# P x V of two heads in one group, in 32-column slices, and its banks in one common ring

## The chip, the cores and the metric

The kernel runs on one core of a Trainium2 chip. The metric is device time in microseconds (us) of one execution; several executions of a kernel are taken and their median is compared. A core has five engines that run their own instruction queues in order and wait for each other through semaphores: TensorE (PE, matrix products; its weight loads are shown as PEld), VectorE (DVE), ScalarE (ACT), GpSimd (POOL) and SyncE (SP, which here issues the DMAs).

## The reference

Attention with a soft cap over 4 x 12 heads of 448 x 64, then two MLPs on 1792 tokens of width 768. The second MLP multiplies two branches, and its last two weights are applied one after the other.

```python
scores = scale * np.matmul(q, k.transpose(0, 1, 3, 2))
scores = cap * np.tanh(scores / cap)
attn = np.exp(scores - np.max(scores, axis=-1, keepdims=True))
attn = attn / (np.sum(attn, axis=-1, keepdims=True) + 1e-09)
x = np.matmul(attn, v)                    # per head; heads side by side: 1792 x 768
h = x @ w_in                              # first MLP, d_ff 2048
x = (h * np.cos(h)) @ w_out
h = (x @ w1) * (x @ w2) @ w3              # second MLP, d_ff 1024
out = h @ w_out2
```

## The kernel before

**Attention.** Heads are taken in 24 pairs. For each head the 448 keys are four chunks of 112, taken two at a time, so a pair has four score blocks. A score block (`c_S`, L615 and L616) is four matmuls into a double bank; ScalarE turns it into tanh and then exp (`c_exp`, L625), and the exponentials land in a tile p of 112 keys x 2 chunks x 448 queries. The ring of p has four tiles. P x V (`c_PV`, L627) is one planned operation for two chunks of both heads, twice per pair. It multiplies with V as the weight (64 columns for each head; the two heads fill the two halves of a bank, L639) and with 32 columns of ones, which gives the sums of the exponentials in a second bank, one strip of 32 partitions for each head and chunk (L643). These matmuls are in plain f32, and the profile shows each of them as two records. `c_move` copies both banks to SBUF (xs and zs), `c_sums` brings the sums together through small DMAs, inverts them (L665) and spreads them over the partitions by way of DRAM, `c_norm` multiplies (x, L369), and `a_out` splits x into a high and a low part for the products that follow, or sends both to DRAM for later.

**Beside it.** In the first part of the attention (until about 190 us) PE also forms the product of the two last weights (`make_w34`, tiles w2 and w3). Then the first MLP starts on the heads that are done (`moe1`): H blocks (xh, xl with wih, wil) give h, a chain on the other engines makes g out of it, and Y blocks (g with woh, wol) are added up in y by DVE, one bank after the other. Every product of this part is three matmuls of split operands (`mm3`, L383 to L385). The second MLP (`moe2`) follows.

**PSUM.** Eight banks: two doubles (four banks) for scores, bank 4 for P x V, bank 5 for the sums, banks 6 and 7 (`hy_r`) for all other products. When attention is over, its banks go to `hy_r`.

**What sets the order.** All operations are recorded in a plan with a due time and with the engines that may run them. `schedule` simulates the engines with fixed costs and picks, at each moment, the ready operation with the earliest due time; a tile of a ring is given out in the order of the ring's queue. The result is one fixed instruction order per engine. Due times of the attention come from `at(g)`, where g counts score blocks: 3.03 us apart for the first 48, then 5.82. P x V of two chunks is due with g at 3 and 5 after the first block of its pair, the copies at 6, `c_norm` at 10 and `a_out` at 11 (lag 9 of its second head, which starts two blocks later).

Of the kernel before, what the change touches and what calls it, by code (L numbers as in the profile page):

```python
# [19 lines left out]
P = 128  # L20
# [52 lines left out]

class Ring:
    def __init__(self, plan, pool, tag, shape, dtype, n, shift=0):
        self.pool, self.tag, self.shape, self.dtype, self.shift = pool, tag, list(shape), dtype, shift
        self.tiles, self.queue = {}, []
        self.free = [(0.0, k) for k in range(n)]
        plan.rings.append(self)
        pool.rings.append(self)  # L80
# [55 lines left out]
class Plan:  # L136
# [57 lines left out]
    def schedule(self):  # L194
# [23 lines left out]
        while done < len(self.ops):  # L218
# [4 lines left out]
            idle = {e for e in free if free[e] <= t + 1e-9}  # L223
            wait, rest, again = {}, [], False
            for c in cands:
# [6 lines left out]
                if pick[0] in idle and port(pick) and free["port"] > t + 1e-9:  # L232
                    pick = None
                elif pick[0] not in idle:
                    if len(o.opts) == 1:
                        wait[pick[0]] = wait.get(pick[0], 0.0) + pick[1] * PAR["back"]
                    pick = None
                if pick is None or any(it.slot is None and it.first is not o for it in o.uses if it.ring) or any(
                        it.ring.queue[0] is not it or not it.ring.free or it.ring.free[0][0] > t + 1e-9
                        for it in o.allocs):  # L240
                    rest.append(c)
                    continue
                for it in o.allocs:
                    it.ring.queue.pop(0)
                    it.slot = heapq.heappop(it.ring.free)[1]
# [88 lines left out]
def program(  # L334
# [70 lines left out]

    class Banks(Ring):
        def __init__(self, slots):
            Ring.__init__(self, plan, pools["psum"], "bank", [P, 512], F32, 0)
            self.free = [(0.0, k) for k in slots]
# [3 lines left out]

    class Doubles(Banks):
        def tile(self, k):
            return doubles[k]
# [42 lines left out]
    if general:  # L459
        s_r, pt_r, pv_r, hy_r = Banks((0, 1)), Banks((2, 3)), Banks((4, 5)), Banks((6, 7))  # L460
    else:
        s_r, pv_r, z_r, hy_r = Doubles((0, 1)), Banks((4,)), Banks((5,)), Banks((6, 7))

# [46 lines left out]
    else:  # L510
        tiles += [("v", [CP, 2, NC, D], F32, 2), ("ones", [CP, Q], F32, 1)]
        tiles += [("p", [CP, 2, S], F32, 4), ("xs", [P, S], F32, 2), ("zs", [P, S], F32, 2), ("rs", [P, 2, S // D], F32, 2), ("rb", [P, S], F32, 1)]
    for tag, shape, dtype, n in tiles:
# [38 lines left out]

    def a_out(i, g):

# [5 lines left out]
        if general:  # L560
            tt(at(g), x, Ref(rb.pop(i // 2)), x, S, ALU.mult, "PD")
        if b < BH:
# [3 lines left out]
        else:  # L566
            th, tl = A["xsh"].ref(), A["xsl"].ref()
        copy(at(g), th, x, S, "PAD")
        lo(at(g), tl, x, th, S)
        if b >= BH:  # L570
            for d, t in zip(xB_d, (th, tl)):
                z = d.at((b, kk), lambda d: d[b - BH, kk])
                dma(at(g + 1), z, t.view(lambda x: x.bitcast(F32)), r=[t], w=[z], kb=230, write=True)

# [52 lines left out]

    def c_PV(n, c, one, g):
        ps = [ph_t.pop((2 * n + j, c)) for j in range(2)]
        if c == 0:  # L630
            pv_t[n], zs_t[n] = pv_r.ref(), z_r.ref()
        pv, z, w = pv_t[n], zs_t[n], Ref(vt[n])
        flags = dict(start=c == 0, stop=c == NT - 1)

        def f():
            for k in range(2):
                first = dict(start=c == 0 and k == 0, stop=c == NT - 1 and k == 1)
                for j, p in enumerate(ps):
                    PE.matmul(pv()[j * D:(j + 1) * D, :S], w()[:, j, 2 * c + k], p()[:, k, :], **first)  # L639
            for j, p in enumerate(ps):  # L640
                for k in range(2):
                    q = Q * (2 * j + k)
                    PE.matmul(z()[q:q + Q, :S], one(), p()[:, k, :], **flags)  # L643

        plan.op(at(g), [("PE", 3 * 4 * MM, f)], r=[w, one, *ps], w=[pv, z])

# [26 lines left out]

    def c_norm(n, g):
        x32[n] = A["x32"].new()
        tt(at(g), Ref(x32[n]), pv_t.pop(n), Ref(rb[n]), S, ALU.mult, "DP")

# [5 lines left out]
    def columns():  # L683
# [3 lines left out]
        for g in range(-8, NT * NH + 16):  # L687
# [3 lines left out]
            if 0 <= g < NT * NH:  # L691
# [12 lines left out]
        plan.move(pv_r, hy_r, at(g))  # L704
        plan.move(z_r, hy_r, at(g))

# [113 lines left out]
    def queries():  # L820
        a_load(0, -2)
        a_split(0, -1)
        for g in range(-8, NC * NH + 24):
# [14 lines left out]
            of_head(a_R, 8, g, NC)  # L838
            of_head(a_out, 17, g, NC)
            if g == NC * G["hsw"] + 11:  # L840
# [513 lines left out]
```

## Time and profile before

| | us |
|---|---|
| median of 3 runs | 1092.33 (1091.08 to 1095.45) |
| the profiled execution | 1093.39 |
| its span in the trace | 1091.1 |
| PE busy | 1064.5 |
| DVE busy | 869.6 |
| ACT busy | 502.1 |
| POOL busy | 161.1 |

The span is the time from the first to the last instruction that was profiled; the execution's own time is 2.3 us more. The mean granted clock of TensorE is 0.997 of full speed. Line numbers are those of the kernel before. A matmul's record lasts longer than the time after which the next one may start, so the cost of a matmul in a row of them is the distance of two starts.

### The profile page before, as it was taken

The page shows a single profiled execution, that of the slowest core. Times are in us where ns is not written, and L with a number is a line of the kernel's source. Part 1 is how long each engine was busy: PE and PEld are TensorE (multiplying, and loading weights), DVE is VectorE, ACT ScalarE, POOL GpSimd, SP SyncE. Part 2 cuts the span into 40 slices and gives each one's busy share as a digit, 9 for nine tenths or more (in the row PEclk, how much of TensorE's full clock was granted, in tenths as well). Part 3 has the DMA queues.
Part 4 walks back from the last instruction along what each step waited for, and adds up shares of the span by engine and source line. Part 5 has one row for each costly group of instructions (what it writes and reads, how often), then busy time and mean ns, then how long its engine had stood idle before and what let it go on. Part 6 is the DMA issues. An engine that isn't in the chain of part 4 may idle for free.

```text
span 1091.1 us, 14889 instructions
## 1 busy us (share of the span) xinstructions
PE 1064.5 (98%) x5424; PEld 892.4 (82%) x5424; DVE 869.6 (80%) x1336; ACT 502.1 (46%) x661; POOL 161.1 (15%) x154
## 2 busy tenths in 40 slices
PE   5999999999999999999999999999999999999997
PEld 3666766677767777779999999998999999999996
DVE  6888767698978988969889977779799879667643
ACT  5788767787666656632244221112333236221121
POOL 2222111122312311111001110001223100000000
PEclk9999999999999999999999999999999999999999
DMA  8796876767756655425643422104655436321232
GB/s 244 200 221 181 231 209 174 219 208 223 219 161 197 188 171 166 153 84 193 223 141 119 147 58 59 58 15 136 223 188 203 141 104 226 119 87 59 59 96 95
DMA packets 83268, 169.17 MB, mean 155 GB/s; under 512 B 19698, under 2 KB 56562, under 8 KB 83186
## 3 DMA queue, kind: packets, MB, share of 16 engines
q1 hardware_dynamic: 83186, 168.14, 51.0%
q8 instruction: 44, 0.72, 0.3%
q14 instruction: 38, 0.31, 0.1%
HBM read 129.30 MB, written 38.62 MB: 154 GB/s over the span
## 4 chain that ended last, share of the span: by engine, by line
PE 90%; DVE 6%; ACT 2%; DMA 1%; issue 1%; SPq 0%; POOL 0%; DVEq 0%; POOLq 0%; ACTq 0%
PE bank L383 25%; PE bank L384 24%; PE bank L385 24%; PE bank L639 6%; PE double L615 3%; PE bank L643 3%; PE double L616 3%; DVE y L369 1%; DVE w L369 1%; DMA wi_d<-wx 1%; ACT double L625 1%; DVE kk L1008 0%; ACT p L625 0%; DMA kr<-in_k 0%; DVE g L369 0%
## 5 line engine op out<-in xcount | busy, mean ns | idle before, releaser
L383 PE MATMUL bank<-g,woh 128*128 128x448 f32 x384 | 140.8, 367 | 4.1 <-DVE y L369 3.5
L384 PE MATMUL bank<-g,woh 128*128 128x448 f32 x384 | 139.4, 363 | 0.9 <-DVE g L369 0.9
L383 PE MATMUL bank<-xh,wih 128*128 128x448 f32 x384 | 140.2, 365 | 0.0
L369 DVE TENSOR_TENSOR y<-bank,y 128x448 f32<-128x448 f32 x168 | 103.5, 618 | 45.7 <-PE bank L385 44.5
L385 PE MATMUL bank<-xh,wil 128*128 128x448 f32 x384 | 139.3, 363 | 0.0
L385 PE MATMUL bank<-g,wol 128*128 128x448 f32 x384 | 139.3, 363 | 0.0
L384 PE MATMUL bank<-xl,wih 128*128 128x448 f32 x384 | 139.2, 363 | 0.0
L359 ACT COPY hs<-bank 128x448 f32<-128x448 f32 x77 | 41.2, 535 | 200.9 <-PE bank L385 200.7
L625 ACT ACTIVATE double<-double,ts 112x896 f32<-112x896 f32 x96 | 94.0, 981 | 69.4 <-PE double L616 69.1
L625 ACT ACTIVATE p<-double,pac 112x896 f32<-112x896 f32 x96 | 96.6, 1012 | 1.8
L383 PEld LDWEIGHTS bank<-g,woh 128*128 128x128 f32 x384 | 71.9, 187 | 20.1 <-DVE y L369 6.2
L615 PE MATMUL double<-qh,ks 128*112 128x448 f32 x192 | 72.6, 378 | 13.9 <-DVE ks L369 9.6
L383 PEld LDWEIGHTS bank<-xh,wih 128*128 128x128 f32 x384 | 71.9, 187 | 16.0 <-issue 8.0
L639 PE MATMUL bank<-p,v 112*64 112x448 f32 x384 | 84.1, 558 | 0.0
L384 PEld LDWEIGHTS bank<-g,woh 128*128 128x128 f32 x384 | 72.1, 188 | 6.4 <-DVE g L369 1.3
L384 PEld LDWEIGHTS bank<-xl,wih 128*128 128x128 f32 x384 | 72.1, 188 | 5.2
L385 PEld LDWEIGHTS bank<-g,wol 128*128 128x128 f32 x384 | 72.1, 188 | 4.2
L385 PEld LDWEIGHTS bank<-xh,wil 128*128 128x128 f32 x384 | 72.1, 188 | 4.2
L616 PE MATMUL double<-ql,ks 128*112 128x448 f32 x192 | 72.3, 376 | 0.0
L384 PE MATMUL bank<-ab,w34h 128*128 128x448 f32 x192 | 69.7, 363 | 0.0
L383 PE MATMUL bank<-ab,w34h 128*128 128x448 f32 x192 | 69.7, 363 | 0.0
L385 PE MATMUL bank<-ab,w34l 128*128 128x448 f32 x192 | 69.3, 361 | 0.0
(224 smaller groups left out, 2304.4 us busy)
## 6 DMA issues: line engine op xcount, KB each, us to landing
rawc<-in_w_out SPq DMA_DIRECT2D x16, 768.0 KB, 5.1
stq<-w_d SPq DMA_DIRECT2D x32, 384.0 KB, 3.3
qr<-in_q SPq DMA_DIRECT2D x48, 224.0 KB, 4.2
kr<-in_k SPq DMA_DIRECT2D x48, 224.0 KB, 4.5
rawc<-in_w_in SPq DMA_DIRECT2D x13, 768.0 KB, 5.4
raw<-in_w3T SPq DMA_DIRECT2D x16, 512.0 KB, 5.9
rawl<-in_w SPq DMA_DIRECT2D x10, 768.0 KB, 4.7
raw<-in_w_out SPq DMA_DIRECT2D x8, 768.0 KB, 7.3
```

The source lines that it names most:

```text
L359: "A": ("ACT", (0.051 if psum else 0.094) + n / 1200, lambda: ACT.copy(dst(), src())),
L369: "D": ("DVE", 0.068 + n / 960, lambda: DVE.tensor_tensor(dst(), a(), b(), op=op))
L383: PE.matmul(out, wh, xh, start=first, stop=False, skip_group_check=on)
L384: PE.matmul(out, wh, xl, start=False, stop=False, skip_group_check=on)
L385: PE.matmul(out, wl, xh, start=False, stop=last, skip_group_check=on)
L615: PE.matmul(o, w, qh(), start=True, stop=False)
L616: PE.matmul(o, w, ql(), start=False, stop=True)
L625: lambda f=f, x=x, o=o: ACT.activation(o(), s(), f, scale=x[:CP]))],
L639: PE.matmul(pv()[j * D:(j + 1) * D, :S], w()[:, j, 2 * c + k], p()[:, k, :], **first)
L643: PE.matmul(z()[q:q + Q, :S], one(), p()[:, k, :], **flags)
```

## The change

Three things change together.

1. P x V of a pair is one operation for all four chunks (`cs` is `[0, 1]`), except for the first two pairs, which keep one operation for every two chunks. V goes in by 32 columns: for each chunk four matmuls (two heads, two halves of V) fill the four strips of a bank, so a pair has 16 V matmuls of 32 columns in place of 8 of 64. The matmuls with ones are the same as before and follow those with V. The planned cost on PE goes from 2.4 to 5.1 us for a whole pair's operation (12 x 2 x 0.2 + 0.3). The p ring has six tiles.
2. Banks 4 to 7 form one ring `hy_r` for P x V, the sums and all other products. In this ring (`loose`) a bank is given to whichever operation is ready, not in the order of the queue; an operation that needs two takes both or waits, and others behind it don't take one from under it (`short`).
3. `c_norm` is due 11 us and `a_out` 14 us after the copies, in place of some steps of g; the DMA of x to DRAM is due 3 us after `a_out`.

```diff
 class Ring:
+    loose = False
...
+                need = {}
+                for it in o.allocs:
+                    need[it.ring] = need.get(it.ring, 0) + 1
+                lack = {r for r, n in need.items() if sum(x[0] <= t + 1e-9 for x in r.free) < n}
                 if pick is None or any(it.slot is None and it.first is not o for it in o.uses if it.ring) or any(
-                        it.ring.queue[0] is not it or not it.ring.free or it.ring.free[0][0] > t + 1e-9
-                        for it in o.allocs):
+                        not r.loose and r.queue[0].first is not o for r in need) or lack or short & need.keys():
+                    short |= {r for r in lack if r.loose}
                     rest.append(c)
                     continue
                 for it in o.allocs:
-                    it.ring.queue.pop(0)
+                    it.ring.queue.remove(it)
...
     class Banks(Ring):
+        loose = not general
...
-        s_r, pv_r, z_r, hy_r = Doubles((0, 1)), Banks((4,)), Banks((5,)), Banks((6, 7))
+        s_r, hy_r = Doubles((0, 1)), Banks((4, 5, 6, 7))
...
-        tiles += [("p", [CP, 2, S], F32, 4), ...
+        tiles += [("p", [CP, 2, S], F32, 6), ...
...
-                dma(at(g + 1), z, t.view(lambda x: x.bitcast(F32)), r=[t], w=[z], kb=230, write=True)
+                dma(due + 3, z, t.view(lambda x: x.bitcast(F32)), r=[t], w=[z], kb=230, write=True)
...
-    def c_PV(n, c, one, g):
-        ps = [ph_t.pop((2 * n + j, c)) for j in range(2)]
-        if c == 0:
-            pv_t[n], zs_t[n] = pv_r.ref(), z_r.ref()
+    def c_PV(n, cs, one, g):
+        ps = {(j, c): ph_t.pop((2 * n + j, c)) for j in range(2) for c in cs}
+        if 0 in cs:
+            pv_t[n], zs_t[n] = hy_r.ref(), hy_r.ref()
         pv, z, w = pv_t[n], zs_t[n], Ref(vt[n])
-        flags = dict(start=c == 0, stop=c == NT - 1)
 
         def f():
-            for k in range(2):
-                first = dict(start=c == 0 and k == 0, stop=c == NT - 1 and k == 1)
-                for j, p in enumerate(ps):
-                    PE.matmul(pv()[j * D:(j + 1) * D, :S], w()[:, j, 2 * c + k], p()[:, k, :], **first)
-            for j, p in enumerate(ps):
-                for k in range(2):
-                    q = Q * (2 * j + k)
-                    PE.matmul(z()[q:q + Q, :S], one(), p()[:, k, :], **flags)
+            for c in range(2 * cs[0], 2 * cs[-1] + 2):
+                flags = dict(start=c == 0, stop=c == NC - 1)
+                for q in range(P // Q):
+                    j, d = divmod(q * Q, D)
+                    PE.matmul(pv()[q * Q:(q + 1) * Q, :S], w()[:, j, c, d:d + Q], ps[j, c // 2]()[:, c % 2, :], **flags)
+            for c in cs:
+                for j in range(2):
+                    for k in range(2):
+                        q = Q * (2 * j + k)
+                        PE.matmul(z()[q:q + Q, :S], one(), ps[j, c]()[:, k, :], start=c == 0, stop=c == NT - 1)
 
-        plan.op(at(g), [("PE", 3 * 4 * MM, f)], r=[w, one, *ps], w=[pv, z])
+        plan.op(at(g), [("PE", 12 * len(cs) * MM + 0.3, f)], r=[w, one, *ps.values()], w=[pv, z])
...
-    def c_norm(n, g):
+    def c_norm(n, due):
...
-            if g >= 3 and g % 2 and g - 3 < NT * NH:
-                c_PV((g - 3) // (2 * NT), (g - 3) % (2 * NT) // 2, one, g)
+            of_two(lambda n, g: n < 2 and c_PV(n, [0], one, g), 3, g)
+            of_two(lambda n, g: c_PV(n, [1] if n < 2 else [0, 1], one, g), 5, g)
             of_two(c_move, 6, g)
             of_two(c_sums, 6, g)
-            of_two(c_norm, 10, g)
-            of_head(a_out, 9, g, NT)
+            of_two(lambda n, g: c_norm(n, at(g) + 11), 6, g)
+            of_two(lambda n, g: a_out(2 * n + 1, at(g) + 14), 6, g)
```

The scheduler makes a new order of everything. On DVE the program of this case goes from 1338 to 1328 instructions, on GpSimd from 158 to 167, on ScalarE from 663 to 664; on PE the 192 V matmuls of 64 columns become 384 of 32.

PE before, one P x V group in the first part of the attention, between a score block (`double`) and the product of weights (`w2h`, `w3h`). The names are tiles with the number of their slot: `bank4` for P x V, `bank5` for the sums, `p2` and `p3` the two exponentials, `v1` the pair's V.

```order
L616 MATMUL double1_83<-ql0_126,ks0_131 112x448
L639 MATMUL bank4_75<-p2_177,v1_128 64x448
L639 MATMUL bank4_75<-p3_188,v1_128 64x448
L639 MATMUL bank4_75<-p2_177,v1_128 64x448
L639 MATMUL bank4_75<-p3_188,v1_128 64x448
L643 MATMUL bank5_76<-p2_177,ones0_109 32x448 x2
L643 MATMUL bank5_76<-p3_188,ones0_109 32x448 x2
L383 MATMUL bank6_77<-w2h0_192,w3h1_316 128x384
```

PE after, a group in the same part, with V in the same slot. "x2" is two matmuls in a row, here the two 32-column halves of one head's V.

```order
L649 MATMUL bank5_76<-p2_177,v1_128 32x448 x2
L649 MATMUL bank5_76<-p3_192,v1_128 32x448 x2
L649 MATMUL bank5_76<-p2_177,v1_128 32x448 x2
L649 MATMUL bank5_76<-p3_192,v1_128 32x448 x2
L649 MATMUL bank5_76<-p0_153,v1_128 32x448 x2
L649 MATMUL bank5_76<-p1_157,v1_128 32x448 x2
L649 MATMUL bank5_76<-p0_153,v1_128 32x448 x2
L649 MATMUL bank5_76<-p1_157,v1_128 32x448 x2
L654 MATMUL bank7_78<-p2_177,ones0_109 32x448 x2
L654 MATMUL bank7_78<-p3_192,ones0_109 32x448 x2
L654 MATMUL bank7_78<-p0_153,ones0_109 32x448 x2
L654 MATMUL bank7_78<-p1_157,ones0_109 32x448 x2
```

The two halves of a pair are now one run of 24 matmuls on four p tiles (`p2`, `p3`, then `p0`, `p1`), 16 with V and then 8 with ones, and the two banks are 5 and 7 in place of 4 and 5.

PE before, the first Y block (`g0`, `woh`, `wol`) in the first MLP, with the H blocks (`xh`, `wih`) on both sides of it.

```order
L383 MATMUL bank6_77<-xh0_507,wih2_1479 128x448
L384 MATMUL bank6_77<-xl0_515,wih2_1479 128x448
L385 MATMUL bank6_77<-xh0_507,wil2_1485 128x448
L383 MATMUL bank7_78<-g0_1773,woh0_1714 128x448
L384 MATMUL bank7_78<-g0_1773,woh0_1714 128x448
L385 MATMUL bank7_78<-g0_1773,wol0_1733 128x448
L383 MATMUL bank7_78<-g0_1773,woh1_1753 128x448
L384 MATMUL bank7_78<-g0_1773,woh1_1753 128x448
L385 MATMUL bank7_78<-g0_1773,wol1_1765 128x448
L383 MATMUL bank6_77<-xh0_507,wih2_1479 128x448
L384 MATMUL bank6_77<-xl0_515,wih2_1479 128x448
L385 MATMUL bank6_77<-xh0_507,wil2_1485 128x448
```

PE after, the first Y blocks, right behind a P x V group (its last rows with ones are shown).

```order
L654 MATMUL bank7_78<-p0_153,ones0_109 32x448 x2
L654 MATMUL bank7_78<-p1_157,ones0_109 32x448 x2
L389 MATMUL bank6_77<-g0_1853,woh0_1820 128x448
L390 MATMUL bank6_77<-g0_1853,woh0_1820 128x448
L391 MATMUL bank6_77<-g0_1853,wol0_1870 128x448
L389 MATMUL bank6_77<-g0_1853,woh1_1856 128x448
L390 MATMUL bank6_77<-g0_1853,woh1_1856 128x448
L391 MATMUL bank6_77<-g0_1853,wol1_1880 128x448
L389 MATMUL bank5_76<-g0_1853,woh0_1820 128x448
L390 MATMUL bank5_76<-g0_1853,woh0_1820 128x448
L391 MATMUL bank5_76<-g0_1853,wol0_1870 128x448
L389 MATMUL bank5_76<-g0_1853,woh1_1856 128x448
```

Before, the Y block has bank 7 and the next H block follows in bank 6, which an earlier H block also filled, so the two banks alternate. After, three Y blocks follow each other in banks 6, 5 and 7 (the third is not shown), with no H block between them, and the first Y block stands behind the P x V group instead of in front of one.

## Rows read from the trace of the kernel before

**Rows 1.** The page: busy us of each engine (share) xinstructions.
```profile
PE 1064.5 (98%) x5424; PEld 892.4 (82%) x5424; DVE 869.6 (80%) x1336; ACT 502.1 (46%) x661; POOL 161.1 (15%) x154
```

**Rows 2.** Three stretches: length, busy us of five engines, PEclk, DMA share, GB/s.
```profile
20.00:50.00 30.00, 26.94 (x141) 17.26 (x140) 23.52 (x31) 22.95 (x32) 7.49 (x7) 0.94 0.75 211
50.00:190.00 140.00, 140.00 (x786) 95.17 (x785) 109.10 (x164) 106.77 (x133) 23.91 (x27) 1.00 0.78 204
190.00:460.00 270.00, 265.69 (x1362) 198.07 (x1361) 231.46 (x340) 185.05 (x212) 61.64 (x54) 1.00 0.64 191
```

**Rows 3.** Waits of PE, 50 to 490 us: total us, times, longest.
```profile
PE bank L383 <- DVE y L369: 3.5, 5, 1.2
PE bank L383 <- DVE y L360: 0.5, 1, 0.5
```

**Rows 4.** The chain that ended last, first and last of 42 such groups.
```profile
38.58 1.65 PE bank L639 x8
...
486.07 0.89 PE bank L643 x8
```

**Rows 5.** V matmuls of the program: xcount, busy us, mean ns.
```profile
L639 PE MATMUL bank<-p,v 112*64 112x448 f32 x384 | 84.1, 558 | 0.0
```

**Rows 6.** Timeline of PE around one group: start us, us, engine, line, operation.
```profile
99.67 0.37 PE L616 MATMUL double<-ql,ks 128*112 128x448 f32 x1
99.97 1.72 PE L639 MATMUL bank<-p,v 112*64 112x448 f32 x8
101.62 0.96 PE L643 MATMUL bank<-p,ones 112*32 112x448 f32 x8
102.51 0.44 PE L383 MATMUL bank<-w2h,w3h 128*128 128x384 f32 x1
102.79 0.34 PE L384 MATMUL bank<-w2l,w3h 128*128 128x384 f32 x1
102.96 0.34 PE L385 MATMUL bank<-w2h,w3l 128*128 128x384 f32 x1
...
104.18 0.37 PE L615 MATMUL double<-qh,ks 128*112 128x448 f32 x1
104.38 0.37 PE L616 MATMUL double<-ql,ks 128*112 128x448 f32 x1
```

**Rows 7.** Timeline of narrow stretches of the same group, PE then PEld.
```profile
100.39 0.55 PE L639 MATMUL bank<-p,v 112*64 112x448 f32 x2
101.14 0.55 PE L639 MATMUL bank<-p,v 112*64 112x448 f32 x2
102.02 0.56 PE L643 MATMUL bank<-p,ones 112*32 112x448 f32 x4
100.39 0.14 PEld L639 LDWEIGHTS bank<-p,v 112*64 112x64 f32 x2 [0.23 <-issue]
101.62 0.16 PEld L643 LDWEIGHTS bank<-p,ones 112*32 112x32 f32 x8 [0.70 <-issue]
```

**Rows 8.** Waits of DVE, 200 to 460 us: total us, times, longest.
```profile
DVE y L369 <- PE bank L385: 11.3, 15, 1.8
DVE hs L360 <- PE bank L385: 3.7, 3, 2.6
DVE zs L360 <- PE bank L643: 3.4, 2, 2.6
```

**Rows 9.** Timeline, DVE and PE: a reciprocal, an x, first use of g.
```profile
201.59 0.20 DVE L665 RECIPROCAL rs<-rs 128x7 f32<-128x7 f32 x1
...
218.93 0.62 DVE L369 TENSOR_TENSOR x<-xs,rb 128x448 f32<-128x448 f32 x1
...
220.46 1.04 DVE L369 TENSOR_TENSOR g<-w,g 128x896 fp32r<-128x896 f32 x1
...
228.29 0.36 PE L383 MATMUL bank<-g,woh 128*128 128x448 f32 x1
```

More of the change, by code (lines that the diff above doesn't have):

```diff
@@ L223, in schedule @@
             idle = {e for e in free if free[e] <= t + 1e-9}
-            wait, rest, again = {}, [], False
+            wait, rest, again, short = {}, [], False, set()
             for c in cands:
@@ L414, in program @@
     class Doubles(Banks):
+        loose = False
         def tile(self, k):
@@ L511, in program @@
         tiles += [("v", [CP, 2, NC, D], F32, 2), ("ones", [CP, Q], F32, 1)]
-        tiles += [("p", [CP, 2, S], F32, 4), ("xs", [P, S], F32, 2), ("zs", [P, S], F32, 2), ("rs", [P, 2, S // D], F32, 2), ("rb", [P, S], F32, 1)]
+        tiles += [("p", [CP, 2, S], F32, 6), ("xs", [P, S], F32, 2), ("zs", [P, S], F32, 2), ("rs", [P, 2, S // D], F32, 2), ("rb", [P, S], F32, 1)]
     for tag, shape, dtype, n in tiles:
@@ L551, in a_split, with a_out @@
             st[i + j] = qh[:, j], ql[:, j], ks[:, j]
-    def a_out(i, g):
+    def a_out(i, due):
         if i % 2 == 0:
@@ L560, in a_out @@
         if general:
-            tt(at(g), x, Ref(rb.pop(i // 2)), x, S, ALU.mult, "PD")
+            tt(due, x, Ref(rb.pop(i // 2)), x, S, ALU.mult, "PD")
         if b < BH:
@@ L567, in a_out @@
             th, tl = A["xsh"].ref(), A["xsl"].ref()
-        copy(at(g), th, x, S, "PAD")
-        lo(at(g), tl, x, th, S)
+        copy(due, th, x, S, "PAD")
+        lo(due, tl, x, th, S)
         if b >= BH:
@@ L672, in c_sums @@
             dma(at(g) + 5, y, lambda k=k: rs_d.item.tile()[n, k].unsqueeze(0).to_broadcast([D, S]), r=[d], w=[y])
-    def c_norm(n, g):
+    def c_norm(n, due):
         x32[n] = A["x32"].new()
-        tt(at(g), Ref(x32[n]), pv_t.pop(n), Ref(rb[n]), S, ALU.mult, "DP")
+        tt(due, Ref(x32[n]), pv_t.pop(n), Ref(rb[n]), S, ALU.mult, "DP")
     def of_two(f, lag, g):
@@ L695, in columns @@
                 c_exp(2 * n + j, c, g)
-            if g >= 3 and g % 2 and g - 3 < NT * NH:
-                c_PV((g - 3) // (2 * NT), (g - 3) % (2 * NT) // 2, one, g)
+            of_two(lambda n, g: n < 2 and c_PV(n, [0], one, g), 3, g)
+            of_two(lambda n, g: c_PV(n, [1] if n < 2 else [0, 1], one, g), 5, g)
             of_two(c_move, 6, g)
             of_two(c_sums, 6, g)
-            of_two(c_norm, 10, g)
-            of_head(a_out, 9, g, NT)
+            of_two(lambda n, g: c_norm(n, at(g) + 11), 6, g)
+            of_two(lambda n, g: a_out(2 * n + 1, at(g) + 14), 6, g)
         first = plan.move(s_r, hy_r, at(g), lambda k: ())
         plan.move(s_r, hy_r, at(g), lambda k: range(4), part_doubles, [first])
-        plan.move(pv_r, hy_r, at(g))
-        plan.move(z_r, hy_r, at(g))
     def v_split(i, g):
@@ L838, in queries @@
             of_head(a_R, 8, g, NC)
-            of_head(a_out, 17, g, NC)
+            of_head(lambda i, g: a_out(i, at(g)), 17, g, NC)
             if g == NC * G["hsw"] + 11:
```

## The prediction

> **What bounds the kernel now.** I read the busy times of the page first: TensorE (PE) is busy for 1064.5 us of the 1091.1 us span, and the next engine, VectorE (DVE), for 869.6 [rows 1]. A share over the whole span says little about one stage, so the table of stretches comes next [rows 2]. From 50 to 190 us, where attention runs beside the product of the two last weights, PE is busy for all 140.00 us and DVE for 109.10. From 190 to 460 us, where attention runs beside the first MLP, PE is busy for 265.69 of 270 and DVE for 231.46. The granted clock is 1.00 in both, the upper of the two levels (2.4 GHz). The list of waits for PE from 50 to 490 us then holds only 4.0 us with a named releaser worth counting: a bank that DVE had yet to empty [rows 3]. And the chain that ended last runs through 42 of the P x V groups one after the other, from the one at 38.58 us to the one that ends near 487 us [rows 4]. So in the whole stretch that the change touches PE sets the pace, and what a P x V group takes on PE is paid one for one. The reader should see that "busy" hides something, though: a busy PE is not a PE at its peak, since a matmul's record overlaps the next one's. What a group costs has to be read from starts, not from busy time.
>
> **What one group costs before.** Each of the 48 groups (24 pairs, two halves) has four f32 matmuls with 64 columns of V and four with 32 columns of ones; each f32 matmul shows as two records (384 for the 192 matmuls of V [rows 5]), so a group has 16 records in 6 passes. Starts are in [rows 6] and, for single passes, in [rows 7].
> - Entry: 99.67 to 99.97 is 0.30, where the same kind of matmul is followed after 0.20 in the regular run (104.18 to 104.38): 0.10 over.
> - The first pass of two abreast, 99.97 to 100.39: 0.42. The next two, 100.39 to 101.14: 0.75, so 0.375 a pass. The first is 0.045 over.
> - The fourth pass until the first pass of ones, 101.14 to 101.62: 0.48, that is 0.105 over, where the width goes from 64 to 32 columns.
> - The first pass of ones, four abreast, 101.62 to 102.02: 0.40, 0.025 over. The second, until the next full-width matmul, 102.02 to 102.51: 0.49, 0.115 over.
> - That first full-width matmul, 102.51 to 102.79: 0.28, against 0.17 for its follower (102.79 to 102.96): 0.11 over.
>
> The group is six passes of 0.375 = 2.25, plus 0.10 + 0.045 + 0.105 + 0.025 + 0.115 + 0.11 = 0.50: 2.75 us. The length repeats along the chain: 1.65 us for the V passes of its first full group, 0.89 for the passes of ones of its last [rows 4].
>
> **P x V in one group, V by 32 columns.** The products stay: two passes, four abreast, in place of four passes, two abreast, for each chunk pair of a head pair. A pair has 8 passes of V and 4 of ones before and after, so 12 x 0.375 = 4.50 us either way. What goes is one entry, one exit and both 64-to-32 changes of width. One group of a pair is 4.50 + 0.10 + 0.025 + 0.115 + 0.11 = 4.85; two groups were 5.50. That saves 0.65 us in each of 22 pairs, 14.3 us. The first two pairs keep two groups, each of six passes in one width: 2.25 + 0.35 = 2.60 instead of 2.75, 0.15 x 4 = 0.6. Together 14.9 us.
>
> Two prices here are not in the trace. First, the step from full width straight to 32 columns: below it lies the 0.10 of 128 to 64, above it the 0.115 + 0.11 of the way back. I take the 0.10, the same direction; the upper end would cost 26 x 0.125 = 3.2 us. Nothing excludes a slightly cheaper step, but with 26 of them even a free one gives only 2.6. Second, a pass of four different slices of V: the passes of two V slices took 0.375, and the first pass of four loads of ones 0.40. I take 0.375, since six quads now follow each other in one width; 0.40 throughout would cost 24 x 12 x 0.025 = 7.2 us. Below 0.375 I see no room, since that pitch is the same at both widths seen.
>
> The number of weight loads doubles for V. They lie under the running pass: the load for the third V pass starts at 100.39 with the pass before it and takes 0.14, and eight loads of ones take 0.16 together [rows 7].
>
> **What the longer group holds up.** It now waits for four exponentials, and everything on PE queues behind it for 4.85 us. The order puts two score blocks of the next pair ahead of it, so its last exponential is two score blocks old when it comes up, and ScalarE has those two blocks to work on meanwhile. The p ring has 6 tiles for that: four for the pair, two for the next. I cost this at nothing; the cover is the 18.4 us that DVE waits for PE and the idle share of ScalarE (185.05 busy of 270) [rows 2, 8]. V's reload into its slot waits for the whole group now; behind it on the SP queue stand the other loads, but the next use of that slot is two pairs away.
>
> **The two banks shared.** Four banks serve all stages except the scores. Before, the bank of Y (the second product of the MLP) had to be emptied by DVE within the one H block that followed; that is the 3.5 + 0.5 = 4.0 us in [rows 3]. After, Y goes round three banks, so most of it should go. Against that, the new group needs two banks free at its start, and the tighter PE leaves DVE less room. I set these two against each other: 0, with -4.0 and +4 as bounds.
>
> **x due a fixed time later.** No instruction is added. In the trace the reciprocal of a pair is done at 201.79, and its x is only formed at 218.93 [rows 9], because the order holds it back. It may come earlier now. Only the first units of the MLP wait for x soon after; later ones read it back long after. I cost it at nothing.
>
> **The sum.** The profiled execution took 1093.39 us (span 1091.1). 1093.39 - 14.9 = 1078.5. The median of the runs shown, 1092.33, lies 1.1 below the profiled one, so the same sum from there is 1077.4. I forecast 1078.
>
> **Rivals.**
> (a) DVE takes over from 190 to 460 us. For it: DVE is busy for 231.46 of 270 there [rows 2], and the order moves the first products of the MLP forward. The first g is ready at 221.50 and is first used at 228.29, a margin of 6.8 us [rows 9]; in the new order 14 pairs lie ahead of it on PE, so PE comes 12 x 0.65 + 0.6 = 8.4 us earlier, which uses such a margin up. Against it: 11.3 + 3.7 + 3.4 = 18.4 us of DVE's idle time are waits for PE [rows 8], and they shrink with PE. 270 - 18.4 = 251.6 is what DVE would need if PE were never late; PE needs 270 - 11 x 0.65 = 262.9. So the cover is 11 us on the mean, but it is not spread evenly. If PE stalls for as much as it gains there (7.2) and once more the 3 or so of present stalls, the time is 1088. The Trainium skill, "TensorEngine Tiling (Array Packing)", section Performance Considerations (PSUM Bottleneck), speaks for this rival: it says that packing speeds up TensorE but not the emptying of PSUM, which may then become the bound.
> (b) Slower: the four slices of V do not run abreast. The place is the 8 passes of V of each pair, 192 in all; it decides against the change from 14.9 / 192 = 0.078 us a pass. If the four loads could not be hidden under the running pass, each pass would grow by the 0.14 of one load [rows 7]: 192 x 0.14 = 27, giving 1105. Against it: ones already go four abreast, in passes of 0.40 and 0.375, with their second loads hidden. The Trainium skill, "TensorE: Matmul & The Clock Gate", section Measured speedup vs the span model, gives 3.07 times for four tiles beside each other, not 4. By that ratio a V pass would take 0.375 x 4 / 3.07 = 0.49, an estimate, 192 x 0.114 = 22 us more, and the time 1100; the quads of ones in this trace do not show such a loss.
> (c) More than the sum: the bank waits go and nothing replaces them, 1078.5 - 4.0 = 1074.5, or 1073.4 from the median.
> (d) The new order stalls somewhere else. The scheduler placed everything anew (DVE has some 10 instructions fewer, GpSimd some 9 more), with due times of the old pace. PE's idle 3.06 us from 20 to 50 us [rows 2] and the start of the MLP are the likely places. A handful of stalls like the 1.2 us ones in [rows 3], eight in number, cost 10: 1088.
>
> **How the numbers follow.** The forecast and its near surroundings (1074 to 1084): 0.62. (c), under 1074: 0.07. (a): 0.17, half of it still faster by over 0.5%. (d): 0.09, mostly within 0.5%. (b): 0.05. About 0.5%, 5.5 us, is what a measurement of this kernel can tell from no change, so the limits are 1086.9 and 1097.8. Faster: 0.62 + 0.07 + 0.09 + 0.01 = 0.79. Within: 0.08 + 0.07 = 0.15. Slower: 0.05 + 0.01 = 0.06. The range goes from 1071 (the banks' 4.0, the median's 1.1 and 2 of the early idle time) to 1089 (7.2 for passes of 0.40 and 3.2 for the dearer step).
>
> **What would show it.** In the profile after: 24 long runs of P x V, 4.6 to 4.7 us from the first V matmul to the next full-width one, without the 0.1 us between V and ones; V passes 0.375 apart. The wait of PE for DVE's y should shrink. Rival (a) would show as waits of PE for g or for weights between 200 and 460 us, and rival (b) as V passes 0.45 apart or more. The forecast is wrong if the groups come out as short as said and the end does not come about 15 us sooner; then the lost time stands in PE's waits.

## The result and the profile after

The changed kernel takes 1078.72 us (median; 1077.02 to 1079.92), the kernel before took 1092.03 beside it: a ratio of 0.9871 [0.9845, 0.9898]. The forecast was 1078. The profiled executions went from 1093.39 to 1077.02 us, their spans from 1091.1 to 1075.2.

The page's busy times, the line that answers to [rows 1]:

```profile
PE 1046.7 (97%) x5808; PEld 897.2 (83%) x5808; DVE 868.7 (81%) x1326; ACT 501.0 (47%) x662; POOL 177.3 (16%) x163
```

PE lost 17.8 us of busy time, DVE 0.9. The three stretches of [rows 2], same columns:

```profile
20.00:50.00 30.00, 26.81 (x163) 18.35 (x162) 26.26 (x33) 23.32 (x32) 9.31 (x8) 0.94 0.83 230
50.00:190.00 140.00, 136.90 (x953) 98.89 (x955) 109.52 (x166) 105.84 (x131) 29.84 (x31) 1.00 0.77 208
190.00:460.00 270.00, 266.00 (x1593) 208.76 (x1586) 238.16 (x346) 186.30 (x214) 72.92 (x60) 1.00 0.64 194
```

What is new is the 136.90: from 50 to 190 us PE was never idle before, and now is for 3.1 us. The waits of PE, 50 to 490 us (total, times, longest), answer to [rows 3]:

```profile
PE bank L389 <- ACT zs L365: 2.7, 2, 2.0
PE double L625 <- ACT p L635: 2.2, 1, 2.2
PE bank L389 <- DVE y L366: 1.2, 1, 1.2
PE bank L391 <- DVE w3l L375: 0.9, 1, 0.9
```

The waits for Y's bank went from 4.0 us to 1.2, and others came: a bank that still holds the sums (`zs`), an exponential, a weight. The waits of DVE, 200 to 460 us, answer to [rows 8]:

```profile
DVE y L375 <- PE bank L391: 9.2, 10, 2.0
DVE wx L883 <- POOL wx L876: 4.5, 2, 4.3
DVE hs L366 <- PE bank L391: 3.3, 3, 1.4
```

In the lines shown DVE waits for PE for 12.5 us, against 18.4 in [rows 8]: its cover shrank, but is not used up. PE's timeline around one group (start, length) answers to [rows 6]:

```profile
100.99 0.34 PE L389 MATMUL bank<-w2h,w3h 128*128 128x384 f32 x1
101.16 0.34 PE L390 MATMUL bank<-w2l,w3h 128*128 128x384 f32 x1
101.34 0.34 PE L391 MATMUL bank<-w2h,w3l 128*128 128x384 f32 x1
101.61 3.21 PE L649 MATMUL bank<-p,v 112*32 112x448 f32 x32
104.64 1.69 PE L654 MATMUL bank<-p,ones 112*32 112x448 f32 x16
106.25 0.45 PE L389 MATMUL bank<-w2h,w3h 128*128 128x384 f32 x1
```

From 101.61 to 106.25 are 4.64 us for twelve passes: 4.50 and 0.14. The weight loads of the same group (PEld) show the passes of four slices of V, to be held against [rows 7]:

```profile
102.01 0.13 PEld L649 LDWEIGHTS bank<-p,v 112*32 112x32 f32 x4 [0.25 <-issue]
102.38 0.13 PEld L649 LDWEIGHTS bank<-p,v 112*32 112x32 f32 x4 [0.25 <-issue]
102.76 0.13 PEld L649 LDWEIGHTS bank<-p,v 112*32 112x32 f32 x4 [0.25 <-issue]
```

They start 0.375 apart: four slices run abreast at the price of two. In the chain that ended last (start, length), whole groups now stand where [rows 4] had halves, but none stands between 223.28 and 321.35 us; there the chain runs through DVE for long pieces, and once through a DMA of 9.50 us that empties the tile which GpSimd fills next:

```profile
57.07 3.14 PE bank L649 x32
...
223.28 1.50 PE bank L654 x16
...
241.37 9.50 DMA wo_d<-wx
...
251.95 1.62 DVE wx L883
...
321.35 3.14 PE bank L649 x32
```

The kernel before had such a stretch too, shorter, from 264 to 304 us, which the prediction passed over when it counted 42 of 48 groups in the chain. Rows of before from that stretch, same columns:

```profile
264.32 1.65 PE bank L639 x8
...
279.00 1.91 DVE kk L1008
...
293.01 1.67 DVE ks L369
...
303.68 1.65 PE bank L639 x8
```

Two more places answer to [rows 9]: a reciprocal with its x, and the first g with its first use on PE:

```profile
203.24 0.20 DVE L676 RECIPROCAL rs<-rs 128x7 f32<-128x7 f32 x1
...
210.06 1.09 DVE L375 TENSOR_TENSOR g<-w,g 128x896 fp32r<-128x896 f32 x1
...
213.34 0.62 DVE L375 TENSOR_TENSOR x<-xs,rb 128x448 f32<-128x448 f32 x1
...
224.72 0.47 PE L389 MATMUL bank<-g,woh 128*128 128x448 f32 x1
```

The margin of g is 224.72 - 211.15 = 13.6 us, twice the 6.8 of before: the new order moved g forward more than PE.

**A balance that the spans obey.** For the profiled execution of each kernel two things are added up over the starts of PE's matmuls. "P x V" is the time that the groups take, from the last matmul ahead of each to the second one behind it, less 0.37 us a group for the two regular distances in it. "Pauses" is every distance between other neighbouring matmuls, less the regular one (0.203, 0.175 or 0.19 us by kind), where more than 0.06 is left; the column after it has those that lie behind 50 us. The rest is the span less P x V and all pauses. Where the granted clock falls, the longer distances count in both columns.

| kernel | P x V | pauses | behind 50 us | span | rest |
|---|---|---|---|---|---|
| before | 133.9 | 18.3 | 8.8 | 1091.1 | 938.9 |
| v32_alone | 126.5 | 20.0 | 10.3 | 1085.4 | 938.9 |
| banks_alone | 133.6 | 9.1 | 0.7 | 1081.2 | 938.5 |
| banks_v32 | 126.3 | 10.9 | 1.1 | 1077.1 | 939.8 |
| two_groups_due | 126.5 | 15.1 | 5.3 | 1080.3 | 938.8 |
| group_alone | 119.0 | 33.5 | 23.5 | 1091.3 | 938.7 |
| after_own_banks | 118.9 | 28.4 | 18.2 | 1085.9 | 938.7 |
| after_old_due | 120.2 | 22.6 | 12.8 | 1081.6 | 938.9 |
| after | 118.8 | 17.2 | 8.8 | 1075.2 | 939.1 |
| after_move_first | 120.8 | 19.5 | 10.0 | 1079.4 | 939.1 |
| after_x3_zs1 | 120.7 | 22.5 | 13.1 | 1081.7 | 938.6 |
| after_turns32 | 119.7 | 18.5 | 9.8 | 1077.1 | 938.9 |
| after_v64 | 123.1 | 12.9 | 3.8 | 1076.7 | 940.7 |
| after_turns64 | 128.6 | 11.6 | 3.1 | 1079.3 | 939.1 |

The rest lies between 938.5 and 939.1 us in all kernels but two, and in these two the first matmul starts later: at 10.9 us in banks_v32 and at 11.2 in after_v64, in the others at 9.6 to 9.8. So the two columns hold nearly all that sets the spans apart. From before to after P x V gave 15.1 us and the pauses 1.1, all of it ahead of 50 us. Behind 50 us the pauses are as long as before, 8.8 us, but they are others. The experiments tell what each part of the change does to the two columns.

### The profile page after: what moved, and what is told of

It is laid out like the page before. It is cut to its first block, busy times and chain, and to the rows that moved or that the text cites. A ratio compares the mean times of both kernels' runs of the same rounds, so it can differ in the third digit from the quotient of the medians.

```text
span 1075.2 us, 15621 instructions
## 1 busy us (share of the span) xinstructions
PE 1046.7 (97%) x5808; PEld 897.2 (83%) x5808; DVE 868.7 (81%) x1326; ACT 501.0 (47%) x662; POOL 177.3 (16%) x163
## 4 chain that ended last, share of the span: by engine, by line
PE 88%; DVE 6%; DMA 2%; ACT 2%; issue 1%; SPq 0%; POOL 0%; DVEq 0%; POOLq 0%; ACTq 0%
PE bank L389 25%; PE bank L390 24%; PE bank L391 24%; PE bank L649 6%; PE double L625 3%; PE double L626 3%; PE bank L654 3%; DMA wo_d<-wx 1%; ACT double L635 1%; DVE wx L883 1%; DVE wx L887 1%; ACT p L635 1%; DMA wi_d<-x 1%; DVE ks L375 0%; DVE w L375 0%
## 5 line engine op out<-in xcount | busy, mean ns | idle before, releaser
L365 ACT COPY hs<-bank 128x448 f32<-128x448 f32 x73 | 39.0, 535 | 180.1 <-PE bank L391 180.0
L389 PEld LDWEIGHTS bank<-g,woh 128*128 128x128 f32 x384 | 72.0, 188 | 13.6 <-ACT zs L365 3.4
L649 PE MATMUL bank<-p,v 112*32 112x448 f32 x768 | 79.0, 547 | 0.0
```

What stands on the lines that cost most here:

```text
L365: "A": ("ACT", (0.051 if psum else 0.094) + n / 1200, lambda: ACT.copy(dst(), src())),
L389: PE.matmul(out, wh, xh, start=first, stop=False, skip_group_check=on)
L649: PE.matmul(pv()[q * Q:(q + 1) * Q, :S], w()[:, j, c, d:d + Q], ps[j, c // 2]()[:, c % 2, :], **flags)
```

## The experiments

Times are medians, with the ratio to the kernel before on the same chip and its 95% interval. Where two kernels are compared, their ratios are subtracted and multiplied by 1092 us. About 0.5% is what can be told from no change, and two kernels whose intervals overlap are not told apart. Every kernel has one profiled execution, and where the scheduler placed the work anew, its order is a new one too.

### The first four: what the group costs

**v32_alone.** The kernel before, V by 32 columns; no other engine's order changes.

```diff
-                for j, p in enumerate(ps):
-                    PE.matmul(pv()[j * D:(j + 1) * D, :S], w()[:, j, 2 * c + k], p()[:, k, :], **first)
+                for q in range(P // Q):
+                    j, d = divmod(q * Q, D)
+                    PE.matmul(pv()[q * Q:(q + 1) * Q, :S], w()[:, j, 2 * c + k, d:d + Q], ps[j]()[:, k, :], **first)
```

> The kernel before with one edit: V goes in by 32 columns, still two groups per pair; the order of every engine stays that of before. Theory W (a change of column width costs PE about 0.1 us): a group's body falls from 2.54 us to 2.39, because the 0.105 between V and ones and the 0.045 after the first V pass go, so 48 groups give 48 x 0.15 = 7.2 us where PE sets the pace: 1092.0 - 7.2 = about 1085. Rival G (the 0.105 is the price of a new bank and new weights, whatever their width): the body stays at about 2.5 us and the time at 1090 to 1092. Rival Q (four different slices of V do not run abreast as well as two): V passes longer than 0.375 us, and the time at 1092 or above.

Measured: 1087.47 us, 0.995 [0.9936, 0.9965]. The body of a group (first V matmul to the next full-width one) went from 2.543 to 2.392 us, 0.15 as forecast for this form; 48 times that is 7.2, and 5.5 us of it arrived (0.005 x 1092).

**after_v64.** The changed kernel with V by 64 columns again; no other engine's order changes.

```diff
-                for q in range(P // Q):
-                    j, d = divmod(q * Q, D)
-                    PE.matmul(pv()[q * Q:(q + 1) * Q, :S], w()[:, j, c, d:d + Q], ps[j, c // 2]()[:, c % 2, :], **flags)
+                for j in range(2):
+                    PE.matmul(pv()[j * D:(j + 1) * D, :S], w()[:, j, c], ps[j, c // 2]()[:, c % 2, :], **flags)
```

> The changed kernel with one edit undone: V by 64 columns again, in the one group of a pair; the order of DVE, ScalarE, GpSimd and the DMAs stays that of the changed kernel. Theory W: each of the 26 groups has one change from 64 to 32 columns, 0.15 us, so the body goes from 4.65 to 4.80 us and the time up by 26 x 0.15 = 3.9 us, to about 1082.6. Rival G: no difference, 1078 to 1079.

Measured: 1078.77 us, 0.9874 [0.9856, 0.9892]; the body is 4.799 instead of 4.648 us. PE does 4.3 us more and the end does not move: the pauses fall by 4.3. What was worth 5.5 us in the old order is worth nothing in the new one that can be told (0.3 us, with intervals of about 2 and 3 us on either side).

**after_turns32 and after_turns64.** V and ones of a chunk pair in turns, so that a group changes its bank and its weights three times instead of once; in the second the width changes too.

```diff
-            for c in range(2 * cs[0], 2 * cs[-1] + 2):
-                flags = dict(start=c == 0, stop=c == NC - 1)
+            for h in cs:
+                for c in range(2 * h, 2 * h + 2):
+                    flags = dict(start=c == 0, stop=c == NC - 1)
...
-            for c in cs:
                 for j in range(2):
                     for k in range(2):
```

> The changed kernel with V and ones taking turns inside the group (two chunks of V, their ones, two chunks of V, their ones), all by 32 columns. Each of the 22 long groups has two more changes of bank and weights, but none of width. Theory W: nothing, body 4.65 us, 1078.7. Rival G (0.1 us for each change of bank and weights): 22 x 2 x 0.1 = 4.4 us more, body 4.85 us, about 1083.

> The same turns with V by 64 columns: the long groups now have three changes of width (64 to 32, back, and again). Theory W: the one change of the V-by-64 kernel, 0.15, and two more of 0.1 to 0.15 each, so the body is 5.0 to 5.1 us and the time 1078.7 + 26 x 0.15 + 22 x (0.2 to 0.3) = 1087 to 1089. Rival G: the same as the 32-column version in turns. With the order of all other engines unchanged, the time should rise by the added PE time one for one if PE sets the pace; if other engines did, it would rise by less than half of it.

Measured: 1079.5 us, 0.9881 [0.9862, 0.9899], body 4.648 as in the changed kernel; and 1081.87 us, 0.9905 [0.989, 0.9921], body 5.087. The timeline of one group of the second (PE, start, length):

```profile
102.99 1.72 PE L649 MATMUL bank<-p,v 112*64 112x448 f32 x8
104.64 0.96 PE L653 MATMUL bank<-p,ones 112*32 112x448 f32 x8
105.53 1.72 PE L649 MATMUL bank<-p,v 112*64 112x448 f32 x8
107.19 0.96 PE L653 MATMUL bank<-p,ones 112*32 112x448 f32 x8
108.08 0.44 PE L389 MATMUL bank<-w2h,w3h 128*128 128x384 f32 x1
```

102.99 to 108.08 is 5.09 for the same twelve passes; the two further changes of width cost 5.087 - 4.799 = 0.29 us against after_v64. Changing bank and weights within one width costs nothing in the body. Of 9.8 us more on PE than in the changed kernel the end shows 3.7, at the edge of what can be told.

### The second four: which part pays

**after_own_banks, after_old_due, group_alone.** Part 2 undone, part 3 undone, and both: the kernel before with the one group of all four chunks, V by 32 and six tiles of p (the DMA of x keeps its new due time, 3 us after the split in place of one step of g; so it does in all kernels here with old due times).

```diff
-        loose = not general
+        loose = False
-        s_r, hy_r = Doubles((0, 1)), Banks((4, 5, 6, 7))
+        s_r, pv_r, z_r, hy_r = Doubles((0, 1)), Banks((4,)), Banks((5,)), Banks((6, 7))
-            pv_t[n], zs_t[n] = hy_r.ref(), hy_r.ref()
+            pv_t[n], zs_t[n] = pv_r.ref(), z_r.ref()
+        plan.move(pv_r, hy_r, at(g))
+        plan.move(z_r, hy_r, at(g))
```

```diff
-            of_two(lambda n, g: c_norm(n, at(g) + 11), 6, g)
-            of_two(lambda n, g: a_out(2 * n + 1, at(g) + 14), 6, g)
+            of_two(lambda n, g: c_norm(n, at(g)), 10, g)
+            of_head(lambda i, g: a_out(i, at(g)), 9, g, NT)
```

> The changed kernel with the second part undone: P x V and the sums keep a bank each (4 and 5), all other products have banks 6 and 7, given out in the order of the queue. Theory A (the prediction: what the shared ring gives back in waits for DVE's y, it takes in new waits): 1078 to 1080, PE's waits for y back at about 4 us and its waits for the copies of the sums (2.7 us in the changed kernel) gone. Rival B (the ring is worth its 4 us of y waits): 1082 to 1083. Rival C (the ring costs more than it gives): 1075 to 1077.

> The changed kernel with the third part undone: x of a pair is formed and split at the due times of before, by steps of g (later, from 190 us on by some 12 us). Theory A (nothing waits for x): 1078 to 1080. Rival B (x is late for the first units of the first MLP, or its DMAs for later ones): 1081 or more, with waits of PE for xh or xl. Rival C (x comes too early in the changed kernel: at 276.44 us ScalarE waits 2.74 us for x with the copy of the sums queued behind it, and PE waits 1.99 us for that copy): 1075 to 1077, the waits for zs gone.

> The kernel before with the first part alone: one group for a pair, V by 32 columns, six p tiles; own banks and due times of before. The PE time it takes away is the whole 14.9 us. Theory A (parts two and three are worth nothing): 1092.0 to 1093.3 less 14.9, 1077 to 1079. Rival B (without the shared ring or the earlier x the gain is lost in waits): 1082 or more.

Measured: 1087.73 us, 0.9949 [0.9935, 0.9964]; 1081.87 us, 0.9897 [0.9879, 0.9914]; and 1093.04 us, 0.9999 [0.9987, 1.001]. The part that shortens PE's work by 15 us gives nothing by itself. The new due times on top of it, still with own banks, give 5.5 us (0.9999 less 0.9949, intervals apart). The waits of PE in group_alone, 20 to 520 us:

```profile
PE bank L389 <- DVE y L375: 7.3, 8, 2.4
PE bank L389 <- DVE sum L375: 3.6, 1, 3.6
...
PE bank L389 <- DVE y L366: 1.9, 1, 1.9
```

With two banks for all other products PE catches up with DVE: 9.2 us of waits for Y's bank against the 4.0 of [rows 3], and one of 3.6 for the bank of a sum of the weights' product. That long one costs twice. Two stretches around it and the whole stretch after it, in group_alone (columns as in [rows 2]; the last three numbers begin with PEclk), and PE's matmuls ahead of it and behind it:

```profile
166.00:170.00 4.00, 0.53 (x2) 0.53 (x3) 2.40 (x4) 1.36 (x2) 1.46 (x2) 0.74 0.04 5
170.00:174.00 4.00, 4.00 (x13) 3.73 (x12) 2.13 (x3) 1.54 (x2) 2.44 (x2) 0.50 0.73 254
...
190.00:460.00 270.00, 260.63 (x1540) 201.31 (x1542) 235.52 (x342) 184.60 (x214) 60.81 (x50) 0.99 0.62 189
```

```profile
163.84 0.33 PE L389 MATMUL bank<-w2h,w3h 128*128 128x384 f32 x1
164.01 0.33 PE L390 MATMUL bank<-w2l,w3h 128*128 128x384 f32 x1
...
170.28 0.52 PE L391 MATMUL bank<-w2h,w3l 128*128 128x384 f32 x1
170.60 0.52 PE L389 MATMUL bank<-w2h,w3h 128*128 128x384 f32 x1
```

After the pause the granted clock is 0.50, the lower level of 1.2 GHz: the products of two weights start 0.32 us apart, where ahead of the pause they start 0.17 apart. From 190 to 460 us PE is busy for 260.63 of 270. This is the outcome of the forecast's rival (a), in the kernel without the shared ring: PE loses as much as its work got shorter (pauses of 33.5 us against 18.3). The sign is not the one that the forecast gave, though; PE waits for banks, not for g or weights.

In after_old_due PE's one large new wait is of another kind (20 to 520 us; then stretches around it):

```profile
PE bank L389 <- ACT zs L365: 3.9, 1, 3.9
```

```profile
279.00:283.00 4.00, 0.36 (x1) 0.36 (x2) 4.00 (x5) 1.41 (x3) 1.54 (x1) 0.76 0.28 107
283.00:287.00 4.00, 4.00 (x12) 3.52 (x12) 2.74 (x5) 0.59 (x2) 1.23 (x1) 0.50 0.38 121
```

What it is shows in the changed kernel's timeline at the same place, where it is 2.0 us long (the bracket is idle time before, and what ended it):

```profile
276.44 0.56 ACT L365 CAST xsh<-x 128x448 fp32r<-128x448 f32 x1 [2.74 <-DVE x L375]
276.91 0.53 ACT L365 COPY zs<-bank 128x448 f32<-128x448 f32 x1
...
277.49 0.48 PE L389 MATMUL bank<-g,woh 128*128 128x448 f32 x1 [1.99 <-ACT zs L365]
```

This is what sharing costs. The next product needs the bank that held the sums; the copy that empties it stands on ScalarE behind a cast, and the cast waits for DVE's x. With banks of their own only the next pair's sums would need that bank. With the new due times x comes sooner there (14.3 us after its reciprocal instead of 17.7), and the wait is 2.0 instead of 3.9 us. The granted clock stays at 1.00 here. That is not a matter of the length alone: in after_turns32 the wait at the same place is 1.81 us, and the clock falls behind it (PE, then the stretch from 279 us):

```profile
278.91 0.47 PE L389 MATMUL bank<-g,woh 128*128 128x448 f32 x1 [1.81 <-ACT zs L365]
```

```profile
279.00:283.00 4.00, 4.00 (x12) 3.54 (x13) 4.00 (x7) 1.96 (x3) 0.82 (x1) 0.57 0.33 118
```

**after_move_first.** The changed kernel, with the two copies that empty the group's banks due three blocks earlier.

```diff
-            of_two(c_move, 6, g)
+            of_two(lambda n, g: c_move(n, g - 3), 6, g)
```

> The changed kernel with one due time moved: the copies of the two banks of P x V are due three steps of g earlier, so the scheduler takes them as soon as the group is done. Theory A (the waits of PE for zs, 2.7 us, are due to copies that stand behind other work on ScalarE): the waits go and the time falls by 2 to 3 us, to about 1076. Rival B (the time lost comes back elsewhere, since DVE has little room): 1078 to 1080, with other waits of the same size.

Measured: 1078.28 us, 0.9865 [0.9847, 0.9883]: level. The wait for `zs` goes, and one for `xs` of 2.7 us comes at 257 us.

### The last four: the parts on their own

**banks_alone.** The kernel before with the shared ring alone: the changed kernel with two groups a pair, V by 64, 4 tiles of p and the old due times.

```diff
-            of_two(lambda n, g: n < 2 and c_PV(n, [0], one, g), 3, g)
-            of_two(lambda n, g: c_PV(n, [1] if n < 2 else [0, 1], one, g), 5, g)
+            of_two(lambda n, g: c_PV(n, [0], one, g), 3, g)
+            of_two(lambda n, g: c_PV(n, [1], one, g), 5, g)
...
-        tiles += [("p", [CP, 2, S], F32, 6), ...
+        tiles += [("p", [CP, 2, S], F32, 4), ...
```

> The kernel before with the second part alone: banks 4 to 7 in one ring; two groups per pair with V by 64 columns, four p tiles and the due times of before. PE's own work is that of before. Theory A (the ring only lets PE run ahead; before, PE already loses just 4 to 6 us to waits for a bank between 50 and 490 us, so there is little to win): 1088 to 1092. Rival B (the ring by itself is worth the 9 us that it is worth under the long groups): 1083 to 1085. The difference would say that the ring is worth its 9 us only because the long, short-cut groups would otherwise stop PE at the two banks.

Measured: 1083.67 us, 0.9919 [0.9901, 0.9937]. PE's work is what it was, and 9.2 us of pauses are gone; behind 50 us 0.7 of 8.8 are left.

**after_x3_zs1.** At 164.75 us in the changed kernel a conversion on GpSimd (`x`, L876) waits 12.13 us for a DMA out of its tile, and the weights' product waits behind it. A third such tile, paid for in memory with one of the two `zs`:

```diff
-    nraw=3, nx=2, w3bufs=2, w2bufs=6,
+    nraw=3, nx=3, w3bufs=2, w2bufs=6,
-... ("zs", [P, S], F32, 2), ...
+... ("zs", [P, S], F32, 1), ...
```

> The changed kernel with three buffers in place of two for the tile x of the first weight conversions (one buffer less for zs, to make room). Theory A (the stall near 168 us, 0.93 us for w3l and 2.17 us for an exponential, starts at GpSimd, which waits 12.13 us for the DMA that empties a buffer of x to DRAM, and from there runs through DVE's 5.19 us wait to PE): that chain goes, PE gains 3 us, 1075 to 1076. Rival B (some other chain is late by as much right behind it): 1078 to 1080, with PE waiting for another operation between 160 and 200 us.

Measured: 1080.34 us, 0.9878 [0.985, 0.9907], between 1073.62 and 1083.91: inconclusive. The conversion still waits (8.72 us), and PE has a pause of 6.6 us there, for an exponential. In banks_alone the same conversion waits 9.20 us and PE does not pause at all, so this wait alone is not what stops PE.

**banks_v32 and two_groups_due.** banks_alone with V by 32 (the edit of v32_alone); and the same with the new due times, which is the changed kernel less its long group.

> The kernel before with the shared ring of four banks, two groups a pair as before, old due times, 4 tiles of p, and V by 32 columns (the run with the ring alone, plus V by 32). Theory A: with the ring and two groups PE is held up by nothing (busy for 140.00 of 140 us and 269.73 of 270 there), so PE's saving of 0.15 us in each of 48 groups is paid in full: 1083.7 - 7.2 = 1076.5 us, and PE's busy time from 190 to 460 us stays above 269. Theory B: under the ring a shorter PE only uncovers the engines behind it, as V by 32 instead of 64 did in the changed kernel (4.3 us less on PE, worth nothing): 1082 to 1084 us, with new waits of PE for DVE or ACT of 5 us or more.

> The changed kernel with two groups a pair for every pair (and 4 tiles of p): part 1's long group undone, V by 32, the ring and the new due times kept. By PE's time alone the two entries and exits a pair come back, 22 x 0.35 = 7.7 us: 1078.7 + 7.7 = 1086 us. Theory A (the long group is what holds PE up, the short ones don't): the 3 us of the new due times come on top of the run with two groups, ring and V by 32: 1073 to 1077 us, faster than the changed kernel or level with it. Theory B (the engines behind PE set the time from here on): level with the changed kernel, 1078 to 1081 us, with waits of PE for DVE or ACT left at 6 us or more from 20 to 520 us.

Measured: 1077.57 us, 0.986 [0.984, 0.9879], and 1081.13 us, 0.9896 [0.9879, 0.9914]. Theory A held for the first: 6.4 us of the 7.2 arrive. Its stretches, 50 to 190 and 190 to 460 us, and its waits of PE, 20 to 520 us:

```profile
50.00:190.00 140.00, 140.00 (x958) 97.55 (x960) 111.56 (x171) 109.24 (x136) 24.39 (x27) 1.00 0.76 208
190.00:460.00 270.00, 269.62 (x1592) 207.19 (x1585) 239.26 (x355) 186.73 (x215) 54.87 (x50) 1.00 0.63 196
```

```profile
PE double L625 <- ACT p L635: 2.4, 2, 2.1
PE bank L390 <- DVE w2l L375: 1.1, 1, 1.1
```

By the first view PE is idle for no more than 0.4 us from 50 to 460 us. So with two groups a pair, V by 32 and the ring PE is full there, and the time is that of the changed kernel. For the second theory A failed: the new due times make two groups slower by 3.9 us (intervals that just touch), with 3.5 us of waits for Y's bank; theory B gave 1078 to 1081. With the long group the same due times gave 5.5 us under own banks; under the ring after_old_due lies 2.8 us above the changed kernel, with intervals that overlap. Nothing that was run beats the changed kernel by more than can be told.

## Why the prediction was right, and where it was not

- **The group.** Right. Forecast 4.85 us with entry and exit, 4.6 to 4.7 for the body; the body is 4.648 (in 22 long groups, not the 24 that the prediction's sign names). The entry straight to 32 columns costs what 128 to 64 did (first V matmul 0.30 us after the last full-width one, both times), and passes of four V slices take 0.375, not the 0.49 of rival (b)'s estimate. Sum over all groups: 14.9 forecast, 15.1 measured. Rival (b) is out.
- **Paid one for one.** This is the step that failed, though the sum came out. The prediction read from [rows 2, 3] that PE sets the pace, so that what a group saves is saved at the end. group_alone has the saving (119.0 in the table) and ends where the kernel before does: pauses rise by 15.2 us. v32_alone, half the saving, got 5.5 of 7.2. A hint stood in the chain of before, from 264 to 304 us.
- **The shared ring at 0.** Mis-sized. The prediction saw in it the 4.0 us of waits and an equal loss against them. Alone it gives 8.8 us (0.0081 x 1092), under the long group 8.5 (0.9949 less 0.9871), and in the two other pairs of kernels that differ by it 9.8 (v32_alone, banks_v32) and 11.1 (group_alone, after_old_due), all outside the bounds of -4.0 and +4. The visible waits were too small a measure. By starts the pauses of before behind 50 us are 8.8 us, and banks_alone has lost 8.1 of them. The list in [rows 3] has 4.0: it ends at 490 us, leaves small pauses out and counts from the end of the last record (at 320.07 us the next matmul starts 1.49 us later instead of 0.20, and the list has 1.1 of it).
- **x due a fixed time later at 0.** Mis-sized for the long group under own banks, where it gave 5.5 us; under the ring the 2.8 gained and, with short groups, the 3.9 lost are at the edge of what can be told. That x comes earlier is true of the pair in [rows 9] (a reciprocal done at 203.44 has its x at 213.34, 9.9 us later and not 17.1), but that pair takes 9.9 us in after_old_due too. Over all 24 pairs the median is 13.5 us, against 14.3 before and 13.6 in after_old_due. So by what way the due times act, beyond the one place at 277 us, is not shown.
- **Rival (a).** It did not come for the whole change, and its time came for the first part alone. Waits of PE for DVE between 200 and 460 us grow as soon as the ring is taken out. The margin of g, by which the prediction argued for it, grew instead; it was banks, not g, that ran short. Yet DVE is near: from 223 to 321 us the chain of the changed kernel runs mostly through it.
- **Rival (d).** In part: two new stalls of 1.1 and 2.3 us at 167 to 172 us and one of 2.2 at 275 are the order's. Behind 50 us the new pauses sum to 8.8 us, as much as the old ones.
- **Why the total fitted.** Two errors met, and that they were of one size is luck. Without the ring 0.1 to 5.6 us of the long group's 15 arrive (group_alone, after_own_banks), and the ring gives more than was set. A shorter way to the same time is not the one the prediction priced: ring and V by 32, with two groups a pair, add up nearly fully (8.8 and 6.4 us). Merging the groups takes 7.5 us from PE's work by the table and brings the end no nearer that can be told. With the old due times the end even comes later with it, and with the two more tiles of p and the new order that it brings: 5.4 us under own banks (v32_alone to group_alone, intervals apart), 4.0 under the ring (banks_v32 to after_old_due, intervals that just touch).

What stays open: why the long group's order has pauses at 165 to 172 and near 257 and 277 us that the short groups' order does not have. They fall differently in each order (in after_x3_zs1 one of 6.6 us, in after_v64 one of 1.8 and one of 1.3); whether it is the burst of 4.65 us on PE or only how the scheduler's costs happen to fall, no run tells apart.

## What to carry to other kernels

"The engine is busy 100%" says that shortening its work can pay, not that it will: ask who is next, by how much, and take an edit away from the finished change as well as adding it to the old kernel; here V by 32 columns was worth 5.5 and 6.4 us with short groups and nothing that can be told under the long one. A buffer count that shows as 4 us of listed waits can be worth twice that: count the pauses between starts, and remember that it also decides whether other savings are paid. When a change joins several edits, price each by itself; here merging the groups brought nothing that V by 32 and the ring did not. Before making bursts longer to save switches, count what the switches cost with the buffers fixed.

## What the runs showed of the hardware

- A pause of TensorE can cost more than its length. After pauses of 3.8 us (group_alone), 4.0 (after_old_due) and 6.6 (after_x3_zs1) the granted clock stood at 0.50 for 5 us after PE had started again (169.4 to 174.6 us in group_alone); after 4.6 us in after_own_banks it was 0.57 from 171 to 175 us. Around 2 us it went either way: after pauses of 2.3 and 2.2 us in the changed kernel it stayed at 1.00, after one of 2.0 us in after_turns32 it was 0.57 from 279 to 283 us. No run here says which length is safe.
- Among narrow f32 passes it is the change of width that costs. Going from 32 columns to 64 and back once more costs 0.29 us (after_turns64 against after_v64), within one width a change of bank and of weights is free: body 4.648 us with one change (the changed kernel) and with three (after_turns32).
- Four matmuls of 32 columns with different weights each run abreast in 0.375 us, the time of two of 64 columns (changed kernel and before); the four weight loads of a pass stay hidden.
